# Eight expert blocks on one Trainium2 core: a smaller block joins the 20-product form, and steps around the first and the last block move

## The chip, the cores and the metric

The kernel runs on one core of a Trainium2 chip, as one program. The metric is the device time of one execution in microseconds (us). Shown is the median of three runs, 371.51 us (370.91 to 371.8). A profile of one execution goes with it; that execution took 370.74 us.

The names used for the engines are those of the profile: PE is TensorE's matmul, PEld its weight load, DVE is VectorE, ACT is ScalarE, POOL is GpSimd, SP is SyncE. L1265 is line 1265 of the kernel before.

## What is computed

A recurrent attention (RWKV) over 4 batches, 8 heads, 768 tokens and head width 48 gives 3072 rows `x` of 384 numbers. They go through a mixture of experts. All of it is float32:

```python
logits = x @ w_gate                       # 8 experts
local = sigmoid(x @ w_local)
# per batch, in order of tokens:
e = argmax(logits[s]) if s == 0 or local[s] < 0.5 else previous e
p = softmax(logits[s])
out[s] = p[e] * (relu(x[s] @ w1[e]) @ w2[e])     # w1[e]: 384 x 1024, w2[e]: 1024 x 384
```

The change lies wholly in the second half, the experts.

## The kernel before, in words

**Units.** The tokens are sorted by expert into ten units of work, each with one expert's `w1` and `w2` (1.5 MB each, loaded whole). Units 0 and 1 (168 slots each) take tokens of the first half of the batches while the router is still busy with the second. Units 2 to 9 are the blocks, one for each expert, with 448, 424, 392, 376, 336, 336, 256 and 192 slots (`BLOCKS`, L43). Unit 2 is called `EARLY` in the code; here it is the first large block. `run` (L1516) issues the units in order, and the order of instructions on each engine is just the order in which `run` calls things: there is no scheduler.

**Stages of a unit.** `gather` (L1148) fetches the token rows by an indirect DMA from POOL's queue, one tile of 128 rows after the other. `turn` (L1163) transposes a tile: three PE transposes into a PSUM bank, then one copy by ACT into `exT`. Then the hidden layer: eight F tiles of 128 hidden units (`FK` = 8), each a sum over three K tiles (`DK` = 3), then relu into `hg`. Then the second layer, then a scaling by the gate and an indirect DMA that scatters the rows into the output.

**The plain hidden layer.** `hidden(i, m)` (L1179) makes one F tile with three matmuls whose moving operand is all the unit's slots, and one relu by ACT (L1187). Each float32 matmul shows as two PE records and two weight loads in the profile, so a block of 256 slots takes 8 x 3 x 2 = 48 records of 256 columns. Two PSUM banks (`hps`) take turns.

**The hidden layer in 20 products.** A unit with at least `PAIRS` slots (L46) is *wide*. `twenty` (L1232) makes four F tiles at a time (g = 0, then g = 1) from 20 products of half the slots in place of 24, at the price of sums: 16 `weight_sums` (DVE, L1222, 128 x 256 each) and 12 `token_sums` (DVE, L1208, half the slots each) which the unit before issues, from `w1` and `exT` of the coming unit. The 20 products come in ten steps, s = 0 to 9, of two products, four records (`STEPS`, `CHAINS`). Step s adds its two products to a PSUM bank, one of two *lanes*; ACT then copies the lane to `snap` (L1268); `settle` (L1226) issues what earlier steps owe: joins on DVE (L1252) that add snaps into `hg`, and relus on ACT (L1257, L1260). Two steps on the same lane follow each other without another lane between them at s = 1, 2 and s = 4, 5.

**What runs amid the steps.** `wide(i, g, s)` (L1564) is called after each step and fills PE's time with other work, by hand-written lists. `fill(*BEHIND[s])` issues products of the second layer: for a block over 192 slots, `seven` (L1304) takes its first 256 slots in 7 products of half size in place of 8 (names "1a" to "7b", two records of 192 columns each) and the slots over 256 as they are (names "r0" to "r3", and "hr"). Those products need `sums` (L1284, DVE, L1291) of `hg` and `factors` (L1293, DVE, L1300) of `w2`. During g = 0 of unit i the products of unit i-1's second half of F tiles are issued, during g = 1 those of unit i's first half. At g = 0, s = 9 `joined(i - 1)` (L1547) issues the sums that end unit i-1, and the load of `w2` for unit i+1 on SP's queue; the load of `w1` for unit i+1 is issued as unit i begins. `turned(i + 1, j)` (L1560) transposes the next unit's tiles. `sent` (L1543) transposes and scatters finished rows of units 0 and 1.

**In the first large block** (i = 2) some lists differ (`i == EARLY`): the next block's four tiles are turned at g = 0, s = 5, 7, 9 and g = 1, s = 1; the four `factors(2, 0)` are made at s = 8 and 9; the 16 weight sums of unit 3 are issued at s = 7, 8, 9 (two each) and in g = 1 at s = 0, 1, 2, 6 (3, 2, 1, 4).

**The last two units.** Unit 8 (256 slots) is not wide and has a branch of its own (L1638): eight times `hidden(8, m)`, and amid them the second-layer products of unit 7's second half. Unit 9 (192 slots) takes `hidden(9, m)` for m = 0 to 7 (L1667); all of unit 8's second layer is issued in its first three turns, and its own second layer (`rows`, L1420, two records of 384 columns each; `half_rows` for the last 64 slots) begins four F tiles behind.

```python
wide=slots >= PAIRS, seven=slots > BLOCKS[-1], rest=max(slots - 2 * P, 0),
...
at = (g * 10 + s - (5 if i == EARLY else 1))
...
if at >= 0 and at % 2 == 0 and at < 8:
    turned(i + 1, at // 2)
```

(The first of these lines is L1084, the others are L1576, L1584 and L1585.)

Of the kernel before, what the change touches and what calls it, by code (L numbers as in the profile page):

```python
# [11 lines left out]
F32 = mybir.dt.float32  # L12
# [8 lines left out]
P = 128  # L21
B, H, S, DH = 4, 8, 768, 48
# [20 lines left out]
BLOCKS = (448, 424, 392, 376, 336, 336, 256, 192)  # L43
HALF = BLOCKS[-1] - P

PAIRS = 336  # L46

FRESH_TO = -1.5 * 2.0 ** -23

# [27 lines left out]

BEHIND = (("r2",), ("1b", "r0", "r1"), ("1a", "2a"), ("6a", "7a"), ("3a", "4a", "5a"), ("r3",), ("2b", "6b"), ("7b", "3b"),
          ("4b", "5b", "hr"), ())


def spread(ap, axis, n):
# [985 lines left out]
class Experts:  # L1068
# [107 lines left out]
        for i in range(n):  # L1176
            self.nc.tensor.transpose(t[:, :P], self.ident, self.ident)

    def hidden(self, i, m):  # L1179
        nc, u = self.nc, self.units[i]  # L1180
        n = u["n"]
        h = self.hps.tile([P, 512], F32, name="h")
        for kk in range(DK):
            nc.tensor.matmul(h[:, :n], lhsT=u["w1"][:, m, kk, :], rhs=u["xT"][:, kk, :],  # L1184
                             start=(kk == 0), stop=(kk == DK - 1))

        nc.scalar.activation(self.kept(i, m), h[:, :n], Act.Relu)  # L1187
# [328 lines left out]
    def run(self, att, flag, ready, free):  # L1516
# [13 lines left out]
        def fill(*names):  # L1530
            for k in names:
                if k in behind:
                    behind.pop(k)()

        def some(steps, k):
            for _ in range(min(k, len(steps))):
                steps.pop(0)()
# [5 lines left out]
        def sent():  # L1543
            if sends:
                self.send(*sends.pop(0))
# [14 lines left out]
        def turned(i, j):  # L1560
            if i < n and j < len(self.units[i]["rows"]):
                self.turn(i, j, self.nc.scalar.copy)

        def wide(i, g, s):  # L1564
            nonlocal behind
            u, r = self.units[i], self.router
            following = self.units[i + 1]["wide"]
            k, z = (i, 0) if g else (i - 1, 1)
            early = k < EARLY
            if s == 0:  # L1570
                behind = {} if early else self.seven(k, z)
                if early:
                    behind = {("1b", "3a")[m - FK + 2]: lambda m=m: self.output(k, m) for m in range(FK - 2, FK)}
            if s in (1, 2) and not early:
                self.sums(k, 2 * z + s - 1)
            at = (g * 10 + s - (5 if i == EARLY else 1))  # L1576
            if (i, g, s) == (EARLY, 0, 2):
                self.routing(2 * FK)
            if (i, g) == (EARLY + 1, 0):
                for when, step in ((1, r.exceeded), (2, lambda: self.flag(0)), (3, lambda: r.halves(0)), (5, lambda: r.halves(E - 1)),  # L1580
                                 (6, lambda: self.flag(1, self.bank("fp"))), (8, lambda: self.flag(2))):
                    if s == when:
                        step()
            if at >= 0 and at % 2 == 0 and at < 8:  # L1584
                turned(i + 1, at // 2)  # L1585
            elif (g, s) in ((0, 9), (1, 1), (1, 3), (1, 5), (1, 7), (1, 9)) and (i, g) > (EARLY, 0):
                sent()
            fill(*BEHIND[s])
            if g == 0:
                if s == 0 and not early:  # L1590
                    fs.extend(self.factors(k, 3))
                if s == (8 if i == EARLY else 3):
                    fs.extend(self.factors(i, 0))
                some(fs, (0, 0, 0, 0, 0, 0, 0, 0, 2, 2)[s] if i == EARLY else (2, 1, 1, 3, 1, 0, 0, 0, 0, 0)[s])
                if s == 5 and following:
                    ws.extend(self.weight_sums(i + 1))
                some(ws, (0, 0, 0, 0, 0, 0, 0, 2, 2, 2)[s] if i == EARLY else (0, 0, 0, 0, 0, 3, 4, 3, 3, 0)[s])
                if i == EARLY and s == 4:
                    drained(k)
                    self.fetch(i + 1, self.nc.sync, 2)  # L1600
                if s == 9 and not early:
                    joined(k)
                    some(js, 3)
                if s == 8:
                    gathered(i + 2, 0, u[2])
            else:
                if s == 0:
                    gathered(i + 2, 1, u[0])
                    some(js, 9)
                some(ends, (0, 0, 1, 1, 0, 0, 0, 0, 0, 0)[s])  # L1610
                if s == 2:
                    fs.extend(self.factors(i, 1))
                    if following:
                        ts.extend(self.token_sums(i + 1))
                if s == 7:
                    fs.extend(self.factors(i, 2))
                some(ws, (3, 2, 1, 0, 0, 0, 4, 0, 0, 0)[s] if i == EARLY else (0, 2, 1, 0, 0, 0, 0, 0, 0, 0)[s])
                some(fs, (0, 0, 1, 3, 0, 0, 0, 1, 2, 1)[s])
                some(ts, (0, 0, 0, 0, 2, 4, 4, 2, 0, 0)[s])
                if s == 5:  # L1620
                    gathered(i + 2, 2, u[6])
                if s == 9:
                    gathered(i + 2, 3, u[6])

        for i in range(n):
# [9 lines left out]
                    self.twenty(i, g, lambda s: wide(i, g, s))  # L1635
                continue

            if u["seven"]:  # L1638

                order = [k for ks in BEHIND for k in ks if k != "hr"]  # L1640
                parts = (0, 1, 4, 8, 12, 15, 18)
                for m in range(FK):
                    if m == 0:
                        self.fetch(i + 1, self.nc.sync, 1)
                        behind = self.seven(i - 1, 1)
                        fs.extend(self.factors(i - 1, 3))
                    self.hidden(i, m)
                    self.settle()
                    if m < 2:
                        self.sums(i - 1, 2 + m)  # L1650
                    some(fs, 4)
                    fill(*order[parts[min(m, 6)]:parts[min(m + 1, 6)]])
                    if m in (2, 3):
                        fs.extend(self.factors(i, m - 2))
                    if m == 5:
                        joined(i - 1)
                        some(js, 9)
                    if m > 5:
                        some(ends, 1)
                    if m in (3, 4):  # L1660
                        turned(i + 1, m - 3)
                    else:
                        sent()
                continue

            lag = 4 if i == n - 1 else 1
            for m in range(FK):  # L1667
                if following and m == FK - 1:
                    turned(i + 1, after - 1)
                self.hidden(i, m)  # L1670
                if (i, m) == (0, 0):
                    att.turn(B * HP - 1, yb[1:])
                if i == n - 1:
                    if m == 0:
                        behind = {**self.seven(i - 1, 0)}
                        for j in range(2):
                            self.sums(i - 1, j)
                        fill(*order)
                        for j in range(2, 4):
                            some(self.factors(i - 1, j), 4)  # L1680
                            self.sums(i - 1, j)
                    if m == 1:
                        behind = self.seven(i - 1, 1)
                        fill(*[k for k in order if k[1] == "a"])
                    if m == 2:
                        fill(*order)
                        joined(i - 1)
                        some(js, 9)
                    if m in (3, 4):
                        some(ends, 1)  # L1690
                if sends and m >= 1 and i > EARLY:
                    self.send(*sends.pop(0))
                if i == n - 1:
                    if m >= lag:
                        self.rows(m - lag)
                elif m >= lag and not (following and m > FK - 3):
                    self.output(i, m - lag)
                if i <= EARLY:
                    self.routing(i * FK + m)
                if i == 0 and m == 1:  # L1700
                    self.fetch(1, self.nc.scalar)
                if m >= FK - after and not (following and m == FK - 1):
                    (turned if following else self.turn)(i + 1, m - (FK - after))
                if following and m == 3:
                    ws.extend(self.weight_sums(i + 1))
                if following and m >= 3:
                    some(ws, 4)
                if following and m >= 4:
                    gathered(i + 2, m - 4, u[m - 1])
# [206 lines left out]
```

## Time and profile before

| what | before |
|---|---|
| median of three runs | 371.51 us (370.91 to 371.8) |
| profiled execution | 370.74 us |
| its span, first to last instruction | 369.0 us |
| mean granted TensorE clock | 0.995 |
| first large block (unit 2), from the trace | 142.87 to 173.62 us |
| units 6 and 7 (336 slots each) | 265.46 to 292.02, 292.02 to 318.20 us |
| unit 8's first plain hidden tile | from 318.35 us |
| unit 9's `half_rows`, the last work of PE | from 358.84 us, for 2.82 us |

Times of the trace count from the span's start; the execution's own time is 1.74 us longer than the span. Rows of the profile give engine, source line, operation, names (output, then inputs), shapes and count. A matmul's shape is weights, then output: `128*128 128x256` is a 128 x 128 weight tile against 256 moving columns. Matmuls are pipelined, so the time that a record costs is the distance to the next one's start and not its own length.

### The profile page before, as it was taken

How to read it: one execution, taken by the hardware profiler on the slowest of the kernel's cores; microseconds unless marked ns; L12 is line 12 of the kernel's file. 1: busy time of each engine (PE TensorE's matmuls, PEld its weight loads, DVE VectorE, ACT ScalarE, POOL GpSimd, SP SyncE). 2: the span in 40 equal slices, each digit the busy share in tenths (PEclk: the TensorE clock that was granted, in tenths of full speed). 3: DMA queues.
4: the chain of work that ended last, by engine and by line, in shares of the span. 5: the costliest groups of instructions: out<-in, count | busy, mean ns of one | idle time of the engine just before them, and what ended most of it. 6: DMA issues, size and time to landing. Idle time of an engine off the chain costs nothing. (4 is left out here: it accounts for less than half of the span.)

```text
span 369.0 us, 9210 instructions
## 1 busy us (share of the span) xinstructions
PE 357.6 (97%) x3542; PEld 309.7 (84%) x3542; DVE 269.5 (73%) x766; ACT 152.3 (41%) x375; POOL 170.5 (46%) x212
## 2 busy tenths in 40 slices
PE   7999999999999999999999999999999999999991
PEld 4776877777769999788989999998998898889971
DVE  6887778788834877598889869879989947536400
ACT  4222232223523124655545557546556545422120
POOL 7689999789522056148374115413504123002022
PEclk9999999999999999999999999999999999999997
DMA  7999999992658656914235516416326416505011
GB/s 241 414 407 408 411 397 375 366 329 103 214 175 298 267 211 255 361 47 147 81 87 203 192 31 228 154 60 234 116 114 234 161 68 226 190 14 215 2 45 37
DMA packets 17381, 74.91 MB, mean 203 GB/s; under 512 B 2395, under 2 KB 6241, under 8 KB 15025
## 3 DMA queue, kind: packets, MB, share of 16 engines
q1 hardware_dynamic: 10336, 56.89, 41.6%
q0 software_dynamic: 3424, 9.48, 7.7%
q10 hardware_dynamic: 3568, 7.87, 5.7%
q8 instruction: 30, 0.49, 0.5%
q14 instruction: 23, 0.18, 0.1%
HBM read 64.79 MB, written 9.47 MB: 201 GB/s over the span
## 5 line engine op out<-in xcount | busy, mean ns | idle before, releaser
L1268 ACT COPY snap<-h 128x336 f32<-128x336 f32 (+4 forms) x120 | 57.7, 480 | 77.7 <-PE h L1265 75.0
L1415 POOL DMA_INDIRECT out_dram<-yo,sid x27 | 33.5, 1239 | 90.6 <-ACT yo L1410 75.3
L1157 POOL DMA_INDIRECT xg<-x_d,gid x29 | 31.5, 1086 | 28.2 <-DVE gid L924 19.3
L1153 POOL COPY seen<-hg 128x1 f32<-128x1 f32 x26 | 16.0, 616 | 54.6 <-ACT hg L1257 50.2
L1252 DVE TENSOR_TENSOR hg<-snap 128x336 f32<-128x336 f32 (+4 forms) x48 | 26.6, 554 | 18.9 <-ACT snap L1268 18.7
L1265 PE MATMUL h<-xs,ws 128*128 128x168 f32 (+4 forms) x192 | 39.4, 328 | 0.0
L1322 PE MATMUL y<-factors,sums 128*128 128x192 f32 x168 | 38.4, 327 | 0.0
L1184 PE MATMUL h<-exT,w1t 128*128 128x168 f32 (+2 forms) x192 | 37.1, 332 | 0.0
L324 DVE TENSOR_TENSOR am<-pair,kept 128x768 f32<-128x768 f32 x32 | 29.9, 952 | 9.7 <-PE pair L314 5.2
L1265 PEld LDWEIGHTS h<-xs,ws 128*128 128x128 f32 x192 | 32.5, 190 | 4.6 <-issue 1.2
L238 POOL TENSOR_TENSOR pd<-rk 128x384 f32<-128x384 f32 x32 | 31.9, 1020 | 7.4 <-PE y L295 4.0
L1184 PEld LDWEIGHTS h<-exT,w1t 128*128 128x128 f32 x192 | 31.0, 190 | 2.7 <-issue 0.5
L1322 PEld LDWEIGHTS y<-factors,sums 128*128 128x128 f32 x168 | 28.6, 190 | 0.1
L1187 ACT ACTIVATE hg<-h 128x168 f32<-128x168 f32 (+2 forms) x32 | 10.7, 334 | 40.0 <-PE h L1184 38.9
L1322 PE MATMUL y<-w2t,hg 128*128 128x192 f32 x112 | 25.0, 328 | 0.0
L1332 PE MATMUL tp<-w2t,hg 128*80 128x384 f32 (+2 forms) x64 | 24.7, 488 | 0.1
L255 POOL TENSOR_TENSOR rw<-rk,tab 128x384 f32<-128x384 f32 x26 | 23.7, 940 | 0.4 <-DMA rk<-in_rk_dram 0.4
L352 ACT COPY xT<-y 128x768 f32<-128x768 f32 x15 | 12.0, 800 | 28.3 <-PE y L344 28.3
L331 PE MATMUL y<-am,kv 128*64 128x128 f32 x360 | 23.0, 277 | 0.0
L234 POOL TENSOR_TENSOR ke<-kv,endT 128x288 f32<-128x288 f32 (+1 forms) x32 | 22.0, 714 | 1.6 <-DMA kv<-in_kv_dram 1.6
L1222 DVE TENSOR_TENSOR ws<-w1t 128x256 f32<-128x256 f32 x48 | 18.8, 417 | 4.2 <-DMA w1t<-in_w_dram 4.2
L1300 DVE TENSOR_TENSOR factors<-w2t 128x192 f32<-128x192 f32 x56 | 19.6, 351 | 2.9 <-PE y L1322 2.9
(293 smaller groups left out, 787.4 us busy)
## 6 DMA issues: line engine op xcount, KB each, us to landing
w1t<-in_w_dram SPq DMA_DIRECT2D x8, 1536.0 KB, 6.9
w2t<-in_w_dram SPq DMA_DIRECT2D x8, 1536.0 KB, 7.0
rk<-in_rk_dram SPq DMA_DIRECT2D x15, 768.0 KB, 10.4
kv<-in_kv_dram SPq DMA_DIRECT2D x16, 584.0 KB, 9.7
vT<-in_vT_dram SPq DMA_DIRECT2D x16, 384.0 KB, 8.5
x_d<-x ACTq DMA_DIRECT2D x4, 1152.0 KB, 10.3
w1t<-in_w_dram SPq DMA_DIRECT2D x2, 768.0 KB, 5.2
w2t<-in_w_dram SPq DMA_DIRECT2D x2, 768.0 KB, 5.1
```

Source lines behind the costliest of these rows:

```text
L238: nc.gpsimd.tensor_mul(t["pd"][:, z], t["rT"][:, z], t["kT"][:, z])
L255: engine.tensor_mul(t["rw"][:, z], t["rT"][:, z], spread(pw, 1, z.stop - z.start))
L324: return lambda: nc.vector.tensor_mul(t["am"][:, g], sc, spread(kept, 1, 2))
L331: nc.tensor.matmul(t["y"][h][p * DP:(p + 1) * DP, c2 * P:(c2 + 1) * P], lhsT=t["v"][:, (2 * c + h) * DH:(2 * c + h) * DH + DP], rhs=t["am" ...
L1157: self.nc.gpsimd.indirect_dma_start(out=xg[:n], out_offset=None, in_=self.x_d[:rows], in_offset=bass.IndirectOffsetOnAxis(ap=u["gid"][:n, ...
L1184: nc.tensor.matmul(h[:, :n], lhsT=u["w1"][:, m, kk, :], rhs=u["xT"][:, kk, :], start=(kk == 0), stop=(kk == DK - 1))
L1252: return lambda: nc.vector.tensor_tensor(o, a, self.snap[:, b, :, :n], op=Alu.add if op == "+" else Alu.subtract)
L1265: nc.tensor.matmul(bank[:, z * n:(z + 1) * n], lhsT=left(a), rhs=right(b), start=(k == 0 and z == 0), stop=(k == len(CHAINS[c]) - 1), skip ...
L1268: nc.scalar.copy(self.snap[:, place, :, :n], source[:, ::-1] if (c, k) in TURNED else source)
L1322: nc.tensor.matmul(bank[:, x * half:(x + 1) * half], lhsT=a(), rhs=b(), start=first, stop=(count(k) == FK // 2), skip_group_check=True)
L1332: nc.tensor.matmul(u["y"][:z, :D], lhsT=u[m][:, 2 * P:2 * P + z], rhs=h[:, m], start=first, stop=last)
L1415: self.nc.gpsimd.indirect_dma_start(out=out.rearrange("n (h d) -> (n h) d", h=2) if half else out, out_offset=bass.IndirectOffsetOnAxis(ap ...
```

## The change

Three things change. `PAIRS` goes from 336 to 256, so unit 8 is wide. The branch for a unit that is not wide but takes `seven` goes (no unit is such any more), and unit 9's part is rewritten: its first two F tiles are made in unit 8's g = 1, s = 0 and 1, in the PSUM bank `tp[1]`, which unit 8 does not use as it has no slots over 256; its other six follow, with unit 8's remaining products spread over them by the new list `LAST`, and its `rows` begin six F tiles behind in place of four. In the first large block, the four turns of the next block's tiles move one step later (g = 0, s = 6, 8, and g = 1, s = 0, 2), `factors(2, 0)` move from s = 8, 9 to s = 6, 7, and the 16 weight sums move to g = 0, s = 9 (two) and g = 1, s = 0, 1, 2, 6 (4, 3, 2, 5). The rows that `sent` handles stay at the same steps.

```diff
-PAIRS = 336
+PAIRS = 256
+
+LAST = {2: ("1b",), 3: ("1a", "2a"), 4: ("6a", "7a", "3a", "4a", "5a", "2b"), 5: ("6b", "7b", "3b", "4b", "5b")}
...
-    def hidden(self, i, m):
+    def hidden(self, i, m, h=None):
...
-        h = self.hps.tile([P, 512], F32, name="h")
+        h = self.hps.tile([P, 512], F32, name="h") if h is None else h
...
-            at = (g * 10 + s - (5 if i == EARLY else 1))
+            at = g * 10 + s - (6 if i == EARLY else 1)
...
-            elif (g, s) in ((0, 9), (1, 1), (1, 3), (1, 5), (1, 7), (1, 9)) and (i, g) > (EARLY, 0):
+            elif (g, s) in ((0, 9), (1, 1), (1, 3), (1, 5), (1, 7), (1, 9)) and (i, g, s) > (EARLY, 1, 2):
                 sent()
             fill(*BEHIND[s])
+            if not u["rest"] and (g, s) in ((1, 0), (1, 1)):
+                self.hidden(i + 1, s, self.tp[1])
...
-                if s == (8 if i == EARLY else 3):
+                if s == (6 if i == EARLY else 3):
                     fs.extend(self.factors(i, 0))
-                some(fs, (0, 0, 0, 0, 0, 0, 0, 0, 2, 2)[s] if i == EARLY else (2, 1, 1, 3, 1, 0, 0, 0, 0, 0)[s])
+                some(fs, (0, 0, 0, 0, 0, 0, 2, 2, 0, 0)[s] if i == EARLY else (2, 1, 1, 3, 1, 0, 0, 0, 0, 0)[s])
...
-                some(ws, (0, 0, 0, 0, 0, 0, 0, 2, 2, 2)[s] if i == EARLY else (0, 0, 0, 0, 0, 3, 4, 3, 3, 0)[s])
+                some(ws, (0, 0, 0, 0, 0, 0, 0, 0, 0, 2)[s] if i == EARLY else (0, 0, 0, 0, 0, 3, 4, 3, 3, 0)[s])
...
-                some(ws, (3, 2, 1, 0, 0, 0, 4, 0, 0, 0)[s] if i == EARLY else (0, 2, 1, 0, 0, 0, 0, 0, 0, 0)[s])
+                some(ws, (4, 3, 2, 0, 0, 0, 5, 0, 0, 0)[s] if i == EARLY else (0, 2, 1, 0, 0, 0, 0, 0, 0, 0)[s])
...
-            if u["seven"]:
...
-            lag = 4 if i == n - 1 else 1
+            lag = 6 if i == n - 1 else 1
             for m in range(FK):
...
-                self.hidden(i, m)
+                if i < n - 1 or m > 1:
+                    self.hidden(i, m)
...
                 if i == n - 1:
-                    if m == 0:
-                        behind = {**self.seven(i - 1, 0)}
-                        for j in range(2):
-                            self.sums(i - 1, j)
-                        fill(*order)
-                        for j in range(2, 4):
-                            some(self.factors(i - 1, j), 4)
-                            self.sums(i - 1, j)
-                    if m == 1:
-                        behind = self.seven(i - 1, 1)
-                        fill(*[k for k in order if k[1] == "a"])
-                    if m == 2:
-                        fill(*order)
-                        joined(i - 1)
-                        some(js, 9)
-                    if m in (3, 4):
+                    if m in (2, 3, 4):
+                        self.settle()
+                    if m == 2:
+                        behind = self.seven(i - 1, 1)
+                        fs.extend(self.factors(i - 1, 3))
+                        some(fs, 4)
+                    if m in (2, 3):
+                        self.sums(i - 1, m)
+                    if m in LAST:
+                        fill(*LAST[m])
+                    if m == 5:
+                        joined(i - 1)
+                        some(js, 9)
+                    if m in (6, 7):
                         some(ends, 1)
```

More of the change, by code (lines that the diff above doesn't have):

```diff
@@ L1636, in run @@
                 continue
-            if u["seven"]:
-                order = [k for ks in BEHIND for k in ks if k != "hr"]
-                parts = (0, 1, 4, 8, 12, 15, 18)
-                for m in range(FK):
-                    if m == 0:
-                        self.fetch(i + 1, self.nc.sync, 1)
+            lag = 6 if i == n - 1 else 1
+            for m in range(FK):
+                if following and m == FK - 1:
+                    turned(i + 1, after - 1)
+                if i < n - 1 or m > 1:
+                    self.hidden(i, m)
+                if (i, m) == (0, 0):
+                    att.turn(B * HP - 1, yb[1:])
+                if i == n - 1:
+                    if m in (2, 3, 4):
+                        self.settle()
+                    if m == 2:
                         behind = self.seven(i - 1, 1)
                         fs.extend(self.factors(i - 1, 3))
-                    self.hidden(i, m)
[L1648 to L1652, printed above, removed]
+                        some(fs, 4)
                     if m in (2, 3):
-                        fs.extend(self.factors(i, m - 2))
+                        self.sums(i - 1, m)
+                    if m in LAST:
+                        fill(*LAST[m])
                     if m == 5:
@@ L1657, in run @@
                         some(js, 9)
-                    if m > 5:
-                        some(ends, 1)
-                    if m in (3, 4):
[L1661 to L1664, printed above, removed]
-            lag = 4 if i == n - 1 else 1
[L1667 to L1674, printed above, removed]
-                        behind = {**self.seven(i - 1, 0)}
-                        for j in range(2):
-                            self.sums(i - 1, j)
-                        fill(*order)
-                        for j in range(2, 4):
-                            some(self.factors(i - 1, j), 4)
-                            self.sums(i - 1, j)
-                    if m == 1:
-                        behind = self.seven(i - 1, 1)
-                        fill(*[k for k in order if k[1] == "a"])
-                    if m == 2:
-                        fill(*order)
-                        joined(i - 1)
-                        some(js, 9)
-                    if m in (3, 4):
+                    if m in (6, 7):
                         some(ends, 1)
```

## The prediction

> **What bounds the kernel now.** I read the page first, then the busy times by stage, then the timeline of PE in the stages that the change touches. The page:
>
> ```profile
> span 369.0 us, 9210 instructions
> ...
> PE 357.6 (97%) x3542; PEld 309.7 (84%) x3542; DVE 269.5 (73%) x766; ACT 152.3 (41%) x375; POOL 170.5 (46%) x212
> ...
> L1184 PEld LDWEIGHTS h<-exT,w1t 128*128 128x128 f32 x192 | 31.0, 190 | 2.7 <-issue 0.5
> ```
>
> PE is busy for 97% of the span. The busy times of four stretches follow: the first large block, unit 6, unit 7, and units 8 and 9 together. After the bounds and the length come PE, PEld, DVE, ACT and POOL, each busy us with its count of instructions, then PE's granted clock.
>
> ```profile
> 142.87:173.62 30.75, 29.72 (x171) 25.64 (x170) 24.85 (x77) 16.33 (x36) 15.21 (x12) 1.00 0.54 209
> 265.46:292.02 26.56, 26.56 (x163) 24.18 (x162) 23.58 (x79) 14.80 (x37) 5.81 (x7) 1.00 0.46 159
> 292.02:318.20 26.18, 26.18 (x159) 23.63 (x158) 16.73 (x54) 14.38 (x36) 5.52 (x7) 1.00 0.43 150
> 318.20:361.40 43.20, 43.20 (x245) 37.54 (x243) 17.46 (x62) 11.17 (x30) 5.83 (x6) 1.00 0.26 95
> ```
>
> In the last three PE is busy for all of the length, at clock 1.00: there only less work for PE saves time. In the first it is idle for 30.75 - 29.72 = 1.03 us by records whose ends are modelled; the distances between their starts show more. PE's timeline there (start, length of the merged records, their count):
>
> ```profile
> 148.53 0.95 PE L1265 MATMUL h<-more,ws 128*128 128x224 f32 x4
> 149.60 0.52 PE L1170 MATMUL tp<-ident,xg 128*128 128x128 f32 x3
> 149.95 0.92 PE L1265 MATMUL h<-xs,ws 128*128 128x224 f32 x4
> 150.71 0.92 PE L1265 MATMUL h<-xs,w1t 128*128 128x224 f32 x4
> 151.97 0.52 PE L1170 MATMUL tp<-ident,xg 128*128 128x128 f32 x3 [0.34 <-DMA xg<-x_d,gid]
> 152.33 0.92 PE L1265 MATMUL h<-xs,w1t 128*128 128x224 f32 x4
> 153.09 0.92 PE L1265 MATMUL h<-xs,ws 128*128 128x224 f32 x4
> 154.34 0.52 PE L1170 MATMUL tp<-ident,xg 128*128 128x128 f32 x3 [0.33 <-DMA xg<-x_d,gid]
> 154.69 0.92 PE L1265 MATMUL h<-exT,w1t 128*128 128x224 f32 x4
> 155.45 0.81 PE L1332 MATMUL tp<-w2t,hg 128*128 128x384 f32 x2
> 156.09 0.92 PE L1265 MATMUL h<-xs,ws 128*128 128x224 f32 x4
> 156.94 0.38 PE L1170 MATMUL tp<-ident,xg 40*128 40x40 f32 x3
> 157.25 0.59 PE L1322 MATMUL y<-w2t,hg 128*128 128x192 f32 x2
> 157.97 1.53 PE L1332 MATMUL tp<-w2t,hg 128*128 128x384 f32 x4
> 159.63 0.65 PE L1265 MATMUL h<-exT,ws 128*128 128x224 f32 x2
> ```
>
> A step's four records cost 0.76 us (149.95 to 150.71), a turn 0.35 (154.34 to 154.69), two records of 384 columns 0.64 (155.45 to 156.09). So PE stands still before the three turns: 148.53 + 0.76 to 149.60 is 0.31 us, 150.71 + 0.76 to 151.97 is 0.50, 153.09 + 0.76 to 154.34 is 0.49. Twice the rows name the arrival of the gathered rows; the first I put down to the same. Two more waits follow. The two records of 192 columns at 157.25 end about 157.58 (0.33, priced below), the next start at 157.97: 0.39. Four of 384 end at 157.97 + 1.28 = 159.25, step 2 starts at 159.63: 0.38. In all 2.07 us. Who holds up the last two is seen on DVE and ACT:
>
> ```profile
> 154.05 0.76 DVE L1222 TENSOR_TENSOR ws<-w1t 128x256 f32<-128x256 f32 x2 [1.90 <-DMA w1t<-in_w_dram]
> ...
> 157.25 1.04 ACT L1257 ACTIVATE hg<-hg 128x448 f32<-128x448 f32 x2 [1.01 <-DVE hg L1252]
> ...
> 159.04 0.53 ACT L1268 COPY snap<-h 128x448 f32<-128x448 f32 x1 [0.75 <-DVE hg L1252]
> ```
>
> DVE stands 1.90 us for the next block's `w1` at the first weight sums. The joins of g = 0 queue behind it; two relus wait for those, and PE's r0 for the relus; the snap of g = 1, s = 1 waits for a join that still reads its place, and step 2 for that snap, as it uses the same lane.
>
> **The change, part by part: unit 8.** The loads and the matmuls of the shortest records on a full weight tile that the experts have (two answers), and rows of unit 8:
>
> ```profile
> 239.16 1.51 PEld L1335 LDWEIGHTS tp<-hg,w2t 128*128 128x128 f32 x12
> ```
>
> ```profile
> 239.16 1.51 PEld L1335 LDWEIGHTS tp<-hg,w2t 128*128 128x128 f32 x12
> ```
>
> ```profile
> 239.32 1.55 PE L1335 MATMUL tp<-hg,w2t 128*128 128x136 f32 x12
> 240.71 0.80 PE L1265 MATMUL h<-exT,ws 128*128 128x188 f32 x4
> ```
>
> ```profile
> 325.79 1.46 PE L1184 MATMUL h<-exT,w1t 128*128 128x256 f32 x6
> ...
> 327.08 0.49 PE L1322 MATMUL mp<-w2t,sums 128*128 128x192 f32 x2
> 327.25 0.35 PEld L1322 LDWEIGHTS y<-factors,hg 128*128 128x128 f32 x2
> 327.29 0.38 ACT L1187 ACTIVATE hg<-h 128x256 f32<-128x256 f32 x1 [2.21 <-PE h L1184]
> 327.41 0.49 PE L1322 MATMUL y<-factors,hg 128*128 128x192 f32 x2
> ```
>
> A record of 256 columns costs (327.08 - 325.79) / 6 = 0.215 us, one of 136 columns (240.71 - 239.32) / 12 = 0.116. On the line through both, 128 columns cost 0.109. Of matmuls with 128 columns against a full weight tile the experts have none; 136 is the nearest. Removed: 48 x 0.215 = 10.32 us. Added: 2 x 20 products of two records, 80 x 0.109 = 8.72. Saved: 1.6 us of PE, in stretches where PE is the bound. All other products of units 8 and 9 stay, only their order moves: 0 on PE.
>
> What could give this back. (a) Weight loads: 80 in place of 48. In the rows above twelve loads take 1.51 us though one is 0.19 long, so they overlap each other and keep 0.116 each; 128 columns ask for 6% more than that, for four to eight records at a stretch before longer ones follow. I take 0. Bound: 0.19 each, the third rival. The Trainium skill ("TensorE: Matmul & The Clock Gate", Part 3, under "The mechanism") says that a weight load runs beside matmuls in flight only where its row group differs, and its LDWEIGHTS section gives columns / 1.2 GHz. By that rule a record here is load and matmul one after the other, an estimate of 0.107 + 0.109 against 0.107 + 0.215, and unit 8 loses 1.8 us (17.3 against 15.5); the trace disagrees, with full-height loads and records both at 0.116 us. These two sentences can be left out.
>
> (b) DVE: unit 7 now issues unit 8's 28 sums. Unit 6 did so for unit 7: 25 instructions more than unit 7 and 23.58 - 16.73 = 6.85 us, 0.27 each. So unit 7 gets 16.73 + 28 x 0.27 = 24.4 us in 26.18, 93% where unit 6 had 89%, and PE never stood in unit 6. I take 0. If that slack is gone, a join comes late as in the first block, where two such waits cost 0.38 each: 0.8 at most. Below zero nothing is to be had, as PE has no idle time there.
>
> (c) Same-lane steps. After a step ACT starts 0.21 us behind PE's last record (327.29 - 327.08) and reads 256 columns in 0.38, so 0.6 us of other work must lie between steps 1 and 2, and 4 and 5. In unit 8's g = 0 these are 1b, r0 and r1, and 3a, 4a, 5a (a product is two records, 327.41 - 327.08 = 0.33): 1.6 and 1.0. In g = 1 unit 8 has no r steps; unit 9's second F tile takes their place, six records of 192 columns at 0.33 / 2 each, 0.99, with 1b 1.3. Covered. That tile overwrites `tp[1]`, from which ACT must have read the first: step 1 and 1b, 4 x 0.109 + 0.33 = 0.77 us, against 0.6. Tight: 0 taken, 0.4 if two relus of unit 8 (0.38 each) are in ACT's queue ahead.
>
> (d) Unit 9. Its tiles 2 to 7 take 0.99 each. The relus that unit 8 still owes are queued on ACT behind tile 2's relu, so sums(8, 2) on DVE ends some 3.5 us after the steps, by my count of the queues; 6a asks for its second sum after three tiles and three products, 3 x 0.99 + 3 x 0.33 = 4.0. Covered by 0.5; if it is not, 0.5 is what a relu and a sum more in the queue would cost. The joining of unit 8 begins three tiles later than before; behind it lie two tiles, all of `rows` (16 records of 384 at 0.32, 5.1 us) and `half_rows`, so its two scatters from POOL are not last. `w1` and `w2` of unit 9 are asked for on SP no later than before in the order of units. 0.
>
> **The first large block.** The turns go behind s = 6, 8 and g = 1, s = 0, 2. The gathered rows come by DMA, issued in unit 1, which nothing here moves: I let the three tiles be usable at 149.60, 151.97 and 154.34 again. Then PE goes: steps 5 and 6 to 148.53 + 1.52 = 150.05; turn, no wait, to 150.40; steps 7, 8 to 151.92; wait 0.05, turn to 152.32; steps 9 and 0 to 153.84; wait 0.50, turn to 154.69; r2 0.64, step 1 0.76, 1b 0.33, r0 and r1 1.28: 157.70. Step 2 started at 159.63 with the fourth turn (156.09 + 0.76 to 157.25 with the changes of shape: 0.40) already done; after the change that turn follows, so the gain is 1.93 - 0.40 = 1.5 us.
>
> This takes the DVE waits as gone: factors (4 x 0.35 at most) and the joins of s = 7 and 8 now run in the 1.90 us in which DVE stood. Weight sums still wait for `w1` at 154.05, but from s = 9 on; behind them is queued only the join of s = 9 (two sums 0.76, so 155.4), which the snap of g = 1, s = 1 needs at 156.3. Relus 0 and 1 follow the snap of g = 1, s = 0 on ACT, 154.0 to about 155.6; r0 comes at 156.42. The weight sums make up the time in g = 1, where the same DVE work as before is left less the 2.6 us moved ahead of 154.05. Bounds of this gain: 0.75 if both DVE waits stay; 2.07 if rows and `w1` land early.
>
> **Sum.** 1.6 + 1.5 = 3.1 us. Profiled execution: 370.74 - 3.1 = 367.6, 1.74 of it outside the span. That execution lay 0.8 under the median of 371.51; for a median I take 371.51 - 3.1 = **368.4 us**.
>
> **Rivals.** *Late joins stay in the first block.* For it: DVE still stands for `w1`, one join behind. Against: a margin of 0.8 us. It gives 371.51 - 1.6 - 0.75 = 369.2. *Unit 8's saving is lost* in waits on ACT and DVE of (b), (c) and (d): 20 snaps and 10 relus take the place of 8 relus, in shorter steps than any wide unit had. Against: unit 7's ACT is busy 14.38 of 26.18 us. It gives 371.51 - 1.5 = 370.0. *The weight loads set the pace* in unit 8 and do not overlap: 80 x 0.19 = 15.2 for 10.3, so 371.51 + 4.9 - 1.5 = 374.9, **slower**. It turns the sign from (10.3 + 1.5) / 80 = 0.148 us a record on; twelve loads at 0.116 speak against. The page named under (a) has this as its rule. *Nothing left:* transfers land later by what PE gains, and unit 8 gains nothing: 371.5. That the change leaves unit 8 alone is no rival: 256 slots meet `slots >= 256`.
>
> **Chances.** Forecast 0.64, late joins 0.14, saving lost 0.10, weight loads 0.05, nothing left 0.07. A measurement of this kernel tells about 0.2%, 0.74 us, from no change. Faster by more 0.88, within 0.07, slower 0.05. The forecast's own range is 367.8 to 369.0; with the two rivals above it, 367.5 to 370.1.
>
> **What the next profile would show.** Right: L1265 with 80 records of 128 columns at 0.109 us, no idle PE from unit 3 on; turns amid the first large block without a wait but for the third; no wait of the snap for a join; DVE's stand for `w1` shorter and later. Wrong: records of 128 columns above 0.148 us apart; PE idle before steps 1 to 2 of unit 8 or before 6a in unit 9; a wait at r0 or at step 2 of the first block; third tile's rows landing after 154.3.

## The result, and the profile after

The changed kernel takes 367.66 us (median of six runs, 366.39 to 368.66); the kernel before, in the same comparison, 371.65 (six runs, 370.27 to 372.51). The ratio of the runs is 0.9896 with a 95% interval of 0.9868 to 0.9924: 3.9 us less, between 2.8 and 4.9. The profiled execution took 367.12 us; before it was 370.74.

The page of the changed kernel:

```profile
span 365.4 us, 9346 instructions
...
PE 355.2 (97%) x3574; PEld 309.9 (85%) x3574; DVE 281.6 (77%) x806; ACT 158.2 (43%) x397; POOL 167.1 (46%) x212
```

PE has 32 records more and is busy 2.4 us less; DVE has 40 instructions more, ACT 22 more. PE still fills 97% of the span. The busy times by stage (bounds, length, then PE, PEld, DVE, ACT, POOL, granted clock) for the first large block, unit 6, unit 7, and units 8 and 9:

```profile
142.08:171.44 29.36, 29.02 (x172) 25.81 (x171) 25.03 (x77) 16.03 (x36) 13.33 (x13) 1.00 0.58 220
263.27:289.84 26.57, 26.57 (x164) 24.20 (x162) 23.60 (x79) 14.78 (x37) 5.82 (x7) 1.00 0.46 161
289.84:316.16 26.32, 26.32 (x161) 23.77 (x160) 24.13 (x81) 14.47 (x36) 5.85 (x7) 1.00 0.42 150
316.16:357.70 41.54, 41.54 (x274) 37.40 (x274) 22.14 (x74) 17.67 (x52) 6.15 (x6) 1.00 0.28 98
```

The last two of the same rows of the kernel before, with bounds drawn at the same records (the first record of each unit, and the start of the last PE record of unit 9):

```profile
292.03:318.35 26.32, 26.32 (x161) 23.77 (x160) 16.87 (x54) 14.38 (x36) 5.52 (x7) 1.00 0.44 152
318.35:361.34 42.99, 42.99 (x244) 37.39 (x242) 17.31 (x62) 11.17 (x30) 5.83 (x6) 1.00 0.26 94
```

Units 8 and 9 lose 1.45 us by these rows (1.43 by unrounded bounds, which the text uses from here on) and have no idle PE. Unit 7 keeps its 26.32 us although its DVE went from 16.87 to 24.13. The first large block goes from 30.75 to 29.36, 1.39 less. The rest of the 3.6 us by which the two spans differ is the moment at which that block begins: 142.87 before, 142.08 after, where nothing ahead of it was changed.

The first large block on PE, on DVE and on ACT (start, length of the merged records, operation, count; in brackets the idle time before and what ended it):

```profile
147.74 0.95 PE L1267 MATMUL h<-more,ws 128*128 128x224 f32 x4
148.53 0.92 PE L1267 MATMUL h<-xs,ws 128*128 128x224 f32 x4
149.29 0.49 PE L1172 MATMUL tp<-ident,xg 128*128 128x128 f32 x3
149.62 1.68 PE L1267 MATMUL h<-xs,w1t 128*128 128x224 f32 x8
151.36 0.52 PE L1172 MATMUL tp<-ident,xg 128*128 128x128 f32 x3
...
152.48 0.92 PE L1267 MATMUL h<-exT,w1t 128*128 128x224 f32 x4
153.67 0.52 PE L1172 MATMUL tp<-ident,xg 128*128 128x128 f32 x3 [0.27 <-DMA xg<-x_d,gid]
...
155.43 0.49 PE L1324 MATMUL y<-w2t,hg 128*128 128x192 f32 x2
155.75 1.45 PE L1334 MATMUL tp<-w2t,hg 128*128 128x384 f32 x4
157.04 0.92 PE L1267 MATMUL h<-exT,ws 128*128 128x224 f32 x4
```

```profile
153.38 0.76 DVE L1224 TENSOR_TENSOR ws<-w1t 128x256 f32<-128x256 f32 x2 [0.81 <-DMA w1t<-in_w_dram]
```

By the starts, with 0.76 us for a step: the first turn waits for nothing (148.53 + 0.76 = 149.29), the second waits 151.36 - 149.62 - 1.52 = 0.22, the third 153.67 - 152.48 - 0.76 = 0.43. Nothing stands before r0 (155.43 + 0.32 = 155.75), and nothing before step 2 (155.75 + 1.28 = 157.03). DVE's stand for `w1` fell from 1.90 to 0.81. From step s = 5 of g = 0 to s = 2 of g = 1 are 157.04 - 147.74 = 9.30 us, where there were 159.63 - 148.53 = 11.10; the fourth turn, 0.40, now comes behind.

### The profile page after: what moved, and what is told of

Read it like the earlier page. It is cut to its first block, busy times and chain, and to the rows that moved or that the text cites. A ratio compares the mean times of both kernels' runs of the same rounds, so it can differ in the third digit from the quotient of the medians.

```text
span 365.4 us, 9346 instructions
## 1 busy us (share of the span) xinstructions
PE 355.2 (97%) x3574; PEld 309.9 (85%) x3574; DVE 281.6 (77%) x806; ACT 158.2 (43%) x397; POOL 167.1 (46%) x212
## 5 line engine op out<-in xcount | busy, mean ns | idle before, releaser
L1270 ACT COPY snap<-h 128x336 f32<-128x336 f32 (+5 forms) x140 | 65.0, 464 | 88.1 <-PE h L1267 83.4
L1267 PE MATMUL h<-xs,ws 128*128 128x168 f32 (+5 forms) x224 | 44.2, 320 | 0.0
L1254 DVE TENSOR_TENSOR hg<-snap 128x336 f32<-128x336 f32 (+5 forms) x56 | 30.0, 536 | 18.2 <-ACT snap L1270 17.8
L1267 PEld LDWEIGHTS h<-xs,ws 128*128 128x128 f32 x224 | 37.2, 190 | 5.2 <-issue 1.4
L1155 POOL COPY seen<-hg 128x1 f32<-128x1 f32 x26 | 12.5, 480 | 52.0 <-ACT hg L1259 47.6
L1224 DVE TENSOR_TENSOR ws<-w1t 128x256 f32<-128x256 f32 x56 | 21.9, 416 | 3.3 <-DMA w1t<-in_w_dram 3.3
L1186 PE MATMUL h<-exT,w1t 128*128 128x168 f32 (+1 forms) x132 | 23.5, 315 | 0.0
L1267 PE MATMUL h<-exT,ws 128*128 128x168 f32 (+5 forms) x112 | 22.1, 319 | 0.0
L1267 PE MATMUL h<-xs,w1t 128*128 128x168 f32 (+5 forms) x112 | 21.8, 319 | 0.0
L333 PEld LDWEIGHTS y<-am,kv 128*64 128x64 f32 x360 | 19.3, 137 | 1.9 <-issue 1.1
```

The costliest lines, as they stand in the source:

```text
L333: nc.tensor.matmul(t["y"][h][p * DP:(p + 1) * DP, c2 * P:(c2 + 1) * P], lhsT=t["v"][:, (2 * c + h) * DH:(2 * c + h) * DH + DP], rhs=t["am" ...
L1254: return lambda: nc.vector.tensor_tensor(o, a, self.snap[:, b, :, :n], op=Alu.add if op == "+" else Alu.subtract)
L1267: nc.tensor.matmul(bank[:, z * n:(z + 1) * n], lhsT=left(a), rhs=right(b), start=(k == 0 and z == 0), stop=(k == len(CHAINS[c]) - 1), skip ...
L1270: nc.scalar.copy(self.snap[:, place, :, :n], source[:, ::-1] if (c, k) in TURNED else source)
```

## The experiments

Each kernel ran beside the kernel before on the same chip. The stage lengths below are in us, from the trace of each; "start" is the start of the first large block. Units 3 to 7 together took 144.72 in every trace, and from the start of the last PE record to the end it is 7.70 or 7.71, so these two columns are left out. Each row is one trace.

| kernel | start | first block | units 8 and 9 | span |
|---|---|---|---|---|
| before | 142.87 | 30.75 | 42.99 | 369.05 |
| again (before, unchanged) | 142.07 | 30.68 | 42.99 | 368.17 |
| unit8 | 141.96 | 31.00 | 41.56 | 366.95 |
| first | 143.61 | 29.08 | 42.99 | 368.11 |
| after | 142.08 | 29.36 | 41.56 | 365.42 |
| turns | 143.12 | 31.30 | 42.99 | 369.84 |
| sums | 142.48 | 29.98 | 42.99 | 367.88 |
| later | 142.80 | 28.82 | 41.56 | 365.60 |
| split2 | 143.49 | 30.69 | 43.35 | 369.96 |
| split4 | 143.56 | 30.21 | 54.03 | 380.23 |
| bare | 143.38 | 28.99 | 43.14 | 367.94 |
| bare_js | 142.13 | 29.45 | 42.81 | 366.82 |

### The two halves apart, and the kernel before once more

`unit8` is the changed kernel with the first large block as it was:

```diff
-            at = g * 10 + s - (6 if i == EARLY else 1)
+            at = (g * 10 + s - (5 if i == EARLY else 1))
...
-                if s == (6 if i == EARLY else 3):
+                if s == (8 if i == EARLY else 3):
...
-                some(ws, (4, 3, 2, 0, 0, 0, 5, 0, 0, 0)[s] if i == EARLY else (0, 2, 1, 0, 0, 0, 0, 0, 0, 0)[s])
+                some(ws, (3, 2, 1, 0, 0, 0, 4, 0, 0, 0)[s] if i == EARLY else (0, 2, 1, 0, 0, 0, 0, 0, 0, 0)[s])
```

and so on for the other lines of that block. `first` is the kernel before with those lines alone taken over. `again` has no edit: it shows how far two traces of one kernel differ.

> The changed kernel with the first large block as before: only unit 8 in 20 products and unit 9's first tiles amid its steps. Theory (two parts that add up, each in its own stage): from unit 8's first step to the last PE record 41.55 us as in the changed kernel (42.99 before), the first large block 30.75 us as before (29.36 in the changed kernel), so 1.4 us under before, a ratio of 0.996. Rival (the start of the first block, 0.8 us earlier in the changed kernel's profile, belongs to the change): over 2 us under before, with the first block starting near 142.1.

> The kernel before with only the first large block's turns, factors and weight sums moved. Theory (two parts that add up): the first block takes 29.4 us in place of 30.75, units 8 and 9 as before 43.0, so 1.4 us under before, a ratio of 0.996. Rival (the earlier start belongs to the change): over 2 us under before. A third way, that unit 8's gain exists only with this one or the other way round, would show as less than 1 us here.

> The kernel before, unchanged, to see how far its stages differ from run to run. Theory (the 0.8 us by which the first block starts earlier in the changed kernel's profile are chance, as the code ahead of it is the same): the start lies somewhere from 141.9 to 143.1, and the stages behind it keep their lengths within 0.1 us: first block 30.75, units 3 to 7 144.7, units 8 and 9 to the last PE record 43.0. Rival (it belongs to the change): 142.87 within 0.2 again.

`unit8` took 369.06 us against 371.17, ratio 0.996 (0.9926 to 0.9993); `first` 369.6, ratio 0.9948 (0.992 to 0.9977). The product of the two, 0.991, agrees with the 0.9896 of both together. In the table the halves do not touch each other: units 8 and 9 are 41.56 with the one and 42.99 with the other. `again` began its first large block 0.80 earlier than the other trace of the same kernel, at 142.07, the changed kernel's own value: this 0.8 us is chance and no gain of the change.

Five traces have the first block as before (30.75, 30.68, 31.00, 30.21, 30.69; mean 30.67), four as after (29.36, 29.08, 28.99, 29.45; mean 29.22). So the block's gain is 1.45 us, with a standard error of some 0.2, and with units 8 and 9 the change is worth 1.45 + 1.43 = 2.9 us by stages.

The scatter within each group has one source, the moment at which transfers land. In all nine traces DVE stands for `w1` before the first weight sums, which start 10.64 to 11.44 us after the block's start. From there to the block's end are 19.57 or 19.58 us in each of the five traces as before, and 18.05 in each of the four as after: at equal landing the change gains 1.52. In `unit8` the first weight sums start 0.08 us behind the third turn, in the other four as before 0.28 to 0.30 ahead of it, and the 19.57 holds all the same. So before the change `w1` decides when the block ends, and not the turns. In the changed ones the third turn, the last for which PE stands, starts 17.77 us before the end in all four; there the two landings keep one distance and can't be told apart.

### What a short record costs

The changed unit 8 saves 1.43 where 1.6 was forecast: (10.32 - 1.43) / 80 = 0.111 us a record, not 0.109. Is that the columns, or the weight load that each record needs? Both kernels leave the computation as it is and cut `hidden`'s matmuls in unit 8 by columns, so that every part loads the same weight tile again; `parts` is 2 in `split2` and 4 in `split4`:

```diff
-        for kk in range(DK):
-            nc.tensor.matmul(h[:, :n], lhsT=u["w1"][:, m, kk, :], rhs=u["xT"][:, kk, :],
-                             start=(kk == 0), stop=(kk == DK - 1))
+        parts = 4 if n == 256 else 1
+        w = n // parts
+        for z in range(parts):
+            for kk in range(DK):
+                nc.tensor.matmul(h[:, z * w:(z + 1) * w], lhsT=u["w1"][:, m, kk, :], rhs=u["xT"][:, kk, z * w:(z + 1) * w],
+                                 start=(kk == 0 and z == 0), stop=(kk == DK - 1), skip_group_check=True)
```

> The kernel before, each plain hidden tile of unit 8 in two parts of 128 columns: 96 records in place of 48, the same columns in all. Theory (a full weight tile can be loaded every 0.112 us, just over the 0.109 us that 128 columns ask for): unit 8 takes 96 x 0.112 = 10.75 us for 10.35, units 8 and 9 43.4 us for 43.0. Rival (the 0.112 us of the changed kernel come from something else in its steps): 0.109 here, 43.1 us.

> The kernel before, each plain hidden tile of unit 8 in four parts of 64 columns: 192 records and as many weight loads in place of 48, the same columns in all. It tells how often a full weight tile can be loaded. Theory (loads overlap one another, but none starts sooner than about 0.11 us behind the one before; 41 of the changed kernel's 80 records of 128 columns are 0.112 us apart): records 0.11 us apart, unit 8 takes 192 x 0.111 = 21.3 us for 10.3, so units 8 and 9 take 54.0 us for 43.0 and the kernel is 11 us slower. Rival (columns alone set the pace): 0.056 us apart, 43.4 us. Rival of the prediction (a load holds up the next for its 0.19 us): 69 us.

The stage of units 8 and 9 in `split2` and in `split4`:

```profile
318.90:362.25 43.35, 43.35 (x290) 39.05 (x290) 17.39 (x62) 11.16 (x30) 5.78 (x6) 1.00 0.26 93
```

```profile
318.49:372.52 54.03, 54.03 (x386) 49.73 (x386) 17.47 (x62) 11.14 (x30) 5.76 (x6) 1.00 0.21 75
```

Only the 48 records of 256 columns at 0.215 changed, 10.32 us in 42.99. 96 records of 128 columns cost 10.32 + 0.36 = 10.68, 0.1113 each; 192 records of 64 columns 10.32 + 11.04 = 21.36, 0.1113 each. Half the columns, the same price. The weight loads of one F tile in `split4`, a full tile of 128 x 128 each, show the pace:

```profile
318.36 2.79 PEld L1187 LDWEIGHTS h<-exT,w1t 128*128 128x128 f32 x24
```

One load is 0.19 long (the prediction's rows), so the 24 follow each other by (2.79 - 0.19) / 23 = 0.113 on average: they overlap. By their single starts the second stands 0.142 behind the first, as the 168-column records ahead set its pace, and the 22 others 0.110 to 0.112 behind the one before. The matmuls themselves can go faster: six of the 192 start only 0.056 to 0.059 us behind the one before. Each is the second record after a longer one, where the first had its load done early and waited. So the loads keep the others 0.111 apart. On the prediction's line through 136 and 256 columns 0.111 belongs to 130 columns. So for a row of short records the two runs show the price of the load, 0.111, at 64 and at 128 columns; between 128 and 136 nothing was measured. The time of `split4` was 381.93 us in one run, 370.56 for the kernel before; `split2` 371.67 beside 370.66.

### The first block: turns alone, sums alone, turns later still

`turns` is the kernel before with the turns one step (two products) later, `sums` the kernel before with factors and weight sums moved. The lines that keep `sent` at its steps, and in `sums` those of the other two lists, are left out:

```diff
-            at = (g * 10 + s - (5 if i == EARLY else 1))
+            at = g * 10 + s - (6 if i == EARLY else 1)
```

```diff
-                if s == (8 if i == EARLY else 3):
+                if s == (6 if i == EARLY else 3):
...
-                some(ws, (0, 0, 0, 0, 0, 0, 0, 2, 2, 2)[s] if i == EARLY else (0, 0, 0, 0, 0, 3, 4, 3, 3, 0)[s])
+                some(ws, (0, 0, 0, 0, 0, 0, 0, 0, 0, 2)[s] if i == EARLY else (0, 0, 0, 0, 0, 3, 4, 3, 3, 0)[s])
```

> The kernel before with the first block's four turns one step later and nothing else: factors and weight sums as before. Theory (DVE's queue, held by the landing of the next block's w1, fixes when r0 and step 2 of g = 1 can go, whenever PE arrives): PE arrives earlier and stands longer at r0, about 1.5 us in place of 0.4, step 2 starts no earlier, and the fourth turn now comes behind it: the block takes 31.1 us, 0.3 more than before. Rival (the prediction's two terms, 0.75 for the turns and 0.75 for the sums, add up): 30.0.

> The kernel before with the first block's factors and weight sums moved, the turns as before. Theory (DVE's queue): the two waits of 0.4 us each at r0 and step 2 go, the three ahead of the turns stay, 1.3 us: the block takes 30.0 us. Rival (the later weight sums are missing further on, as DVE is the busier engine of g = 1): 30.8 or more, with waits of PE for joins in g = 1 or at the start of unit 3.

`turns` took 370.84 us against 370.56, ratio 0.9993 (0.9966 to 1.0021): no gain. `sums` 369.9, ratio 0.9975 (0.9951 to 0.9998). Their block lengths against the mean of 30.67 are +0.6 and -0.7, one trace each: together they would make -0.1, and the pair in one kernel makes -1.45. Traces of one kind of block differ by up to 0.8, which is less than that gap. Where `turns` loses it, on DVE, ACT and PE:

```profile
154.35 0.76 DVE L1222 TENSOR_TENSOR ws<-w1t 128x256 f32<-128x256 f32 x2 [2.48 <-DMA w1t<-in_w_dram]
```

```profile
157.54 1.04 ACT L1257 ACTIVATE hg<-hg 128x448 f32<-128x448 f32 x2 [2.51 <-DVE hg L1252]
```

```profile
156.39 0.49 PE L1322 MATMUL y<-w2t,hg 128*128 128x192 f32 x2
158.26 1.53 PE L1332 MATMUL tp<-w2t,hg 128*128 128x384 f32 x4 [1.38 <-ACT hg L1257]
159.93 1.02 PE L1265 MATMUL h<-exT,ws 128*128 128x224 f32 x4
```

PE comes to r0 sooner and stands 158.26 - 156.39 - 0.33 = 1.54 us, then 159.93 - 158.26 - 1.28 = 0.39 before step 2. The relus that r0 needs wait for joins, and the joins queue on DVE behind weight sums that stand 2.48 us for `w1`. `w1` does not land earlier for PE being earlier (154.35 here with a start at 143.12, so 11.23 us behind it; 154.05 and 142.87 before, 11.18). While the sums stand ahead of the joins, r0 can't come earlier, and a wait that vanishes before a turn reappears before r0. Step 2 starts 16.81 us after the block's start, where it was 16.76, and the fourth turn, 0.40, now comes behind it: that is the block's loss. From the first weight sums to the block's end are 20.07 us, 0.50 more than before.

In `sums` the other half is seen: the turns wait nearly as before, r0 and step 2 hardly.

```profile
148.14 0.95 PE L1265 MATMUL h<-more,ws 128*128 128x224 f32 x4
149.24 0.52 PE L1170 MATMUL tp<-ident,xg 128*128 128x128 f32 x3
...
150.35 0.92 PE L1265 MATMUL h<-xs,w1t 128*128 128x224 f32 x4
151.64 0.52 PE L1170 MATMUL tp<-ident,xg 128*128 128x128 f32 x3 [0.36 <-DMA xg<-x_d,gid]
...
156.85 0.59 PE L1322 MATMUL y<-w2t,hg 128*128 128x192 f32 x2
157.28 1.45 PE L1332 MATMUL tp<-w2t,hg 128*128 128x384 f32 x4
158.57 0.92 PE L1265 MATMUL h<-exT,ws 128*128 128x224 f32 x4
```

The first turn waits 149.24 - 148.14 - 0.76 = 0.34, the second 151.64 - 150.35 - 0.76 = 0.53; r0 only 157.28 - 156.85 - 0.33 = 0.10, step 2 nothing (157.28 + 1.28 = 158.56). DVE does not stand for `w1` here. The waits of the turns end with the rows' landing: the trace has the first two tiles landed at 149.11 and 151.50, 0.13 and 0.14 us before their turns.

`later` takes the changed kernel and sets the turns so that no gathered tile is late (the line that keeps `sent` at its steps is left out):

```diff
+LATER = ((0, 6), (0, 9), (1, 1), (1, 2))
...
-            if at >= 0 and at % 2 == 0 and at < 8:
+            if i == EARLY:
+                if (g, s) in LATER:
+                    turned(i + 1, LATER.index((g, s)))
+            elif at >= 0 and at % 2 == 0 and at < 8:
```

> The changed kernel with the first block's second and third turn later again: behind g = 0, s = 9 and g = 1, s = 1 in place of g = 0, s = 8 and g = 1, s = 0. Theory (what is left of PE's standing there, 0.25 and 0.43 us, is the rows' landing alone, and work exists to put ahead of it): the first block takes 28.7 us in place of 29.36, with no wait ahead of any turn; 0.7 us under the changed kernel, so near 3.5 under before. Rival (DVE or ACT then sets the end of the block, as their work is the same): 29.2 or more, with a wait of PE at r0, at step 2, or at the end of g = 1.

```profile
150.34 1.68 PE L1269 MATMUL h<-xs,w1t 128*128 128x224 f32 x8
151.94 1.02 PE L1269 MATMUL h<-xs,ws 128*128 128x224 f32 x4
152.80 0.49 PE L1174 MATMUL tp<-ident,xg 128*128 128x128 f32 x3
153.12 0.92 PE L1269 MATMUL h<-exT,w1t 128*128 128x224 f32 x4
```

The waits before the turns are gone, but step 9 costs 152.80 - 150.34 - 1.52 = 0.94 in place of 0.76. It shares its lane with step 7, whose copy on ACT runs from 151.35 to 151.88 and for which step 9's weight loads wait 0.27 us; the turn that stood between 8 and 9 had covered that copy. The block is 28.82, some 0.4 under the mean of the changed ones. The time, 367.36 us with a ratio of 0.9892 (0.9854 to 0.993), can't be told from the changed kernel's 0.9896.

### Unit 8 without unit 9's tiles amid its steps

`bare` gives unit 9 its first two F tiles back at their own place, behind unit 8's steps; all else stays changed:

```diff
-            if not u["rest"] and (g, s) in ((1, 0), (1, 1)):
-                self.hidden(i + 1, s, self.tp[1])
...
-                if i < n - 1 or m > 1:
-                    self.hidden(i, m)
+                self.hidden(i, m)
```

> The changed kernel with unit 9's first two F tiles behind unit 8's steps and not amid them, in the ordinary banks. Theory (a lane needs 0.6 us between two steps on it): between steps 1 and 2 of unit 8's g = 1 lies only product 1b, 0.33 us, so PE stands 0.3 us there and nowhere else; units 8 and 9 take 41.85 us for 41.56. Rival (what stands between is hidden, as ACT is quick): 41.56. Other rival (relus and sums that unit 8 owes come late as well): 42.2 or more.

Units 8 and 9 took 43.14: 1.58 more than the changed kernel, and 0.15 more than before the change. The 0.3 us that was expected is far too little. The steps s = 0 to 2 of g = 1, in the changed kernel and then in `bare`:

```profile
328.60 0.61 PE L1267 MATMUL h<-exT,w1t 128*128 128x128 f32 x4
329.04 1.14 PE L1186 MATMUL tp<-exT,w1t 128*128 128x192 f32 x6
...
330.02 0.61 PE L1267 MATMUL h<-xs,ws 128*128 128x128 f32 x4
...
330.46 0.49 PE L1324 MATMUL y<-w2t,hg 128*128 128x192 f32 x2
...
330.79 1.14 PE L1186 MATMUL tp<-exT,w1t 128*128 128x192 f32 x6
330.88 0.37 ACT L1270 COPY snap<-h 128x256 f32<-128x256 f32 x1 [0.27 <-DVE hg L1254]
...
331.77 0.61 PE L1267 MATMUL h<-exT,ws 128*128 128x128 f32 x4
```

```profile
329.53 0.61 PE L1267 MATMUL h<-exT,w1t 128*128 128x128 f32 x4
...
330.16 0.71 PE L1267 MATMUL h<-xs,ws 128*128 128x128 f32 x4
...
330.63 0.74 DVE L1394 TENSOR_TENSOR t<-y,t 128x192 f32<-128x192 f32 x2
...
330.77 0.59 PE L1324 MATMUL y<-w2t,hg 128*128 128x192 f32 x2
331.29 0.41 DVE L1254 TENSOR_TENSOR hg<-snap 128x256 f32<-128x256 f32 x1
...
331.81 0.37 ACT L1270 COPY snap<-h 128x256 f32<-128x256 f32 x1 [0.58 <-DVE hg L1254]
...
332.24 0.71 PE L1267 MATMUL h<-exT,ws 128*128 128x128 f32 x4 [0.87 <-ACT snap L1270]
```

In `bare`, with 0.45 for a step and 0.33 for a product of two records, PE stands before step 1 (330.16 - 329.53 - 0.45 = 0.18), before 1b (330.77 - 330.16 - 0.45 = 0.16) and before step 2 (332.24 - 330.77 - 0.33 = 1.14): 1.48 of the 1.58. The last is a chain of three: step 2 uses the lane of step 1; the snap of that lane must not overwrite a place that the join of step 9 still reads; that join is queued on DVE behind sums (L1394) that finish unit 7's rows. In the changed kernel the snap waits for the join just the same, at 330.88, and ends at 331.25, but PE has unit 9's second tile to do from 330.79 to 331.77.

`bare_js` tests that chain: `bare`, with the three sums of unit 7 issued one step later.

```diff
-                    some(js, 3)
+                    some(js, 3 if i < n - 2 else 0)
```

> As bare (unit 9's first tiles not amid unit 8's steps), and in unit 8 the first three of the seven sums that end unit 7 are issued one step later, behind the join of step 9 in place of ahead of it. Theory (in bare PE stood 1.1 us before step 2 since the snap of step 1 overwrites what the join of step 9 reads, and that join was queued on DVE behind the three sums): the join runs some 0.9 us earlier, PE stands 0.3 us or less before step 2 and a little longer before product 1b, which needs the bank that the first of the sums frees; units 8 and 9 take 42.2 us for bare's 43.1. Rival (the lane alone needs that time, the join has nothing to do with it): 43.1 again.

```profile
329.36 0.71 PE L1267 MATMUL h<-xs,ws 128*128 128x128 f32 x4
...
330.09 0.59 PE L1324 MATMUL y<-w2t,hg 128*128 128x192 f32 x2
...
330.75 0.71 PE L1267 MATMUL h<-exT,ws 128*128 128x128 f32 x4
...
331.95 0.61 PE L1267 MATMUL h<-xs,ws 128*128 128x128 f32 x4
...
332.65 0.92 PE L1324 MATMUL y<-factors,sums 128*128 128x192 f32 x4
```

The wait before step 2 fell from 1.14 to 330.75 - 330.09 - 0.33 = 0.33, so the chain caused 0.81 of it. Units 8 and 9 won only 0.33, though, to 42.81 and not the 42.2 expected: 1b now waits 330.09 - 329.36 - 0.45 = 0.28, and 6a 332.65 - 331.95 - 0.45 = 0.25 for its sums, which come behind the moved ones on DVE. In single runs `bare` took 369.78 us beside a median of 370.56 for the kernel before, `bare_js` 368.73 beside 370.66.

## Why the prediction held, and where its steps were off

**The sum.** 3.1 us were forecast; stage by stage the change is worth 2.9, and the timings say 3.9 with an interval of 2.8 to 4.9. The time of 367.66 lies 0.7 under the forecast 368.4, which is 0.14 below the forecast's own range (367.8 to 369.0) and inside the one with the two rivals (367.5 to 370.1). Of the same size is the chance in the start of the first block, 0.8 in the two traces. The stages do not show the 1.0 us by which 3.9 exceeds 2.9. It lies within the interval, and what it is stays open; the prediction has no term for it.

**Unit 8's records: right kind, wrong by 0.002.** The step that drew a line through 136 and 256 columns and read it at 128 gave 0.109; the runs give 0.1113. At 128 columns the weight loads already set the pace, by that little. It cost 0.17 us of the 1.6. The bound of (a), loads at 0.19, was far off: they overlap. The rule of the Trainium skill that was weighed there ("TensorE: Matmul & The Clock Gate", Part 3, "The mechanism") would have put a record at 0.216; the trace disagrees. The same section also lets a load into the background weight buffer be pulled ahead of matmuls in flight, which the prediction did not weigh, and with which the overlap seen here agrees. The Trainium skill's section "LDWEIGHTS (loading the stationary operand)" on that page gives, as an estimate for a load of 128 columns, 128 / 1.2 GHz = 0.107 us. Taken as the least distance of two records it comes close to the 0.111 that `split2` and `split4` show; the length of one load in the trace, 0.19, differs.

**(b) DVE in unit 7: right.** 24.13 us against 24.4 forecast, in 26.32, with no idle PE.

**(c) Same-lane steps: right in its end, wrong in its reason and price.** Covered, and the tight place held: ACT's relu of unit 9's first tile ends 0.18 before the second tile needs the bank.

```profile
330.28 0.33 ACT L1189 ACTIVATE hg<-tp 128x192 f32<-128x192 f32 x1
```

But the step counted 0.6 us from step 1 to step 2 (ACT's start and its copy), and missed that the copy itself waits for a join behind unit 7's sums. The 1.3 us that it had put there sufficed by their margin. From step 1's last record to the end of its snap are 331.25 - 330.46 = 0.79 here and 332.18 - 330.61 = 1.57 in `bare`. The prediction gave no price for the cover being gone (its 0.4 is for the first tile's bank being read late); `bare` shows 1.58, more than unit 8 saves. The two tiles are no detail of the change: without them the 20 products gain nothing in unit 8 as the lists stand, and 0.18 us with unit 7's sums moved (`bare_js`, 42.81 for 42.99).

**(d) Unit 9: right.** 7.70 us from the start of the last PE record to the end, 7.71 before; no PE wait in unit 9.

**The first block: size right, terms not separate.** Forecast 1.5, measured 1.45 by means and 1.52 at equal landing of `w1`. The wait of the third turn was 0.43 (0.50 forecast), that of the second 0.22 (0.05 forecast), as the tile was usable 9.28 us after the block's start in place of 9.10. The waits at r0 and step 2 went, as the step said. What it did not say is that its terms hold only together: the bound of 0.75 "if both DVE waits stay" counted the turns' gain as kept in that case. `turns` is that case, with the weight sums in their old place, and the gain is none, since what PE saves ahead of r0 it then waits there. The prediction's 2.07 us of waits were not five prices to add: before the change the chain from `w1` over the joins to r0 and step 2 set the block's end, and the waits ahead of the turns lay beside it. The rival of late joins, at 369.2, was priced at least 0.75 too low by the same slip.

**The rivals.** Weight loads as the pace: in part true, at 0.111 and not 0.19, and so without effect on the sign. Unit 8's saving lost: not with unit 9's tiles as cover, but wholly without them (`bare`). Nothing left: units 3 to 7 kept 144.72 us to the hundredth, so no transfer took anything back in them.

## What to carry to other kernels

Before cutting matmuls into more and shorter ones, ask what each new record must load: here 64 columns cost as much as 128, since each record brought a full weight tile and those came 0.111 us apart. When several waits stand one behind the other and a transfer ends the last one, removing an early one only moves the time to the next; price such edits as a chain, not as a sum. A stage whose length varies from trace to trace, but not when it is counted from a landing, names its chain by that. And when moved work is called cover, follow the whole chain that it covers, on every engine's queue, for what of that chain is then left uncovered is the price if the cover goes.

## What was not expected of the hardware

Loads of a full 128 x 128 float32 weight tile, each 0.19 us long, overlap and in `split4` follow each other 0.110 to 0.112 us apart, and matmuls of 64 and 128 columns then cost the same 0.111 us on average, though six records of 64 columns, behind one that had waited with its load done, follow by 0.056 to 0.059. And two parts of one program vary very differently from trace to trace: the first large block begins anywhere from 141.96 to 143.61 us with the same instructions ahead of it, while the following five units, 144.72 us long, agree to 0.01 in twelve traces. The first block's own length varies by up to 0.8 us, all of it with the moment at which its transfers land.
